# A recurrence with a mixture of experts on one core: the last two experts summed straight to 128 rows, the last weight loaded in two parts, the first output units in halves

## The chip, the cores and the metric

The kernel runs on one core of a Trainium2 chip. A core has five engines with instruction streams of their own: TensorE (PE, matmuls), VectorE (DVE), ScalarE (ACT), GpSimd (POOL) and SyncE (SP). They wait for one another by semaphores. Sixteen DMA engines move data between the memory outside (HBM) and the core's memory, of 128 partitions. Matmuls write to PSUM. The metric is the device time of one execution in microseconds (us), the median over several runs.

## The reference

Inputs are `x` and `f_logit` of shape (4, 5056, 256), a vector `lower_bound` of 256, `phi` (256 x 32), `w1` (8 x 256 x 1024) and `w2` (8 x 1024 x 256), all in fp32. The first part is a gated recurrence along the sequence, the second a soft mixture of 8 experts with 4 slots each:

```python
f = lower_bound + (1 - lower_bound) * sigmoid(f_logit)
for t in range(S):
    h = f[:, t] * h + (1 - f[:, t]) * x[:, t]
    y[:, t] = h
x = y.reshape(20224, 256)
logits = x @ phi                               # 20224 x 32
d = softmax(logits, axis=0)                    # over all tokens
slot_input = (d.T @ x).reshape(8, 4, 256)
slot_out[e] = relu(slot_input[e] @ w1[e]) @ w2[e]
c = softmax(logits, axis=1)                    # over the 32 slots
out = c @ slot_out                             # 20224 x 256
```

The slot inputs are sums over all tokens, so no output can be computed before the whole sequence has been read and all experts have run.

## The kernel before

The tokens are worked on in units: `n_grp` = 10 groups along the sequence, for each of `B` = 4 sequences, make 40 units of 512 tokens (448 in the units of the last group but one). In a unit a partition holds `R` = 4 neighbouring tokens, so one partition's piece of a unit in `out` is 4 KB in a row. The order of the instructions is written out by hand; each engine runs its own in that order.

**First stage** (the loop at L336). Units are loaded by SyncE, gated (ACT), multiplied (POOL), transposed (PE), scanned (DVE), transposed back and multiplied with `phi`. The exponentials of the logits stay on chip in `etall`, with one block of 32 partitions for each sequence b. Their weighted sum of tokens goes to `slot_ps`.

**Weights.** `load_w` (L104) issues the 16 weight loads on POOL, `w1` first and then `w2`, one expert each. POOL's DMAs read fp32 and write bf16: 1 MB read and 512 KB written for each load. `W_AT` (L111) says at which unit how many are issued; the last eight, all of `w2`, come at unit 36. In the built program a load waits for the landing of the load eight before it.

**Experts** (L411 to L489). `hid` (L416) holds the hidden activations, transposed, with 32 columns for each expert: the expert's own 4 slots are filled and the other 28 columns are zero. It is cleared by POOL (L417), after the loads in POOL's order, and filled from the transposes by ACT (L467, experts 0 to 3) and DVE (L469, experts 4 to 7). At L478 a loop over the experts and over the 8 chunks `fc` of 128 hidden values multiplies them with `w2`:

```python
nc.tensor.matmul(so4_ps[ds(fc % 4 * NS, NS), :], hid[:, fc, e], w2_sb[e][:, fc], ...)
```

The 32 rows of result go to one of four blocks of rows of `so4_ps`, by `fc % 4`. The four partial sums have then to be added, and the 32 rows repeated for the four sequences. That is what `rep` does: a matrix of 128 x 128 with a one wherever row and column agree modulo 32. DVE copies `so4_ps` to `so4` (L486), PE multiplies it with `rep` in fp32 (L488), and DVE divides by the softmax sums and writes `slot_out` in bf16 (L489): 128 rows, the 32 slots once for each sequence.

**Output** (L496 to L518). For each unit four matmuls (L502) take the 32 rows of its sequence and write four tokens for each partition to PSUM (`op`, four buffers). Then either DVE, in one instruction (L508), or ACT, in four (L514), multiplies with the reciprocal row sums `rrow` and writes `ob` (six buffers). Two counters, `load_dve` and `load_act`, say which of the engines takes a unit. SyncE issues one DMA of 512 KB for each unit (L516).

Of the kernel before, what the change touches and what calls it, by code (L numbers as in the profile page):

```python
# [10 lines left out]
BF16 = mybir.dt.bfloat16  # L11
AX = mybir.AxisListType
ALU = mybir.AluOpType
ACT = mybir.ActivationFunctionType
# [4 lines left out]
def kernel(  # L19
# [10 lines left out]
    nc = tc.nc  # L30
    B, S, D = x.shape
    E = moe_w1.shape[0]
    F = moe_w1.shape[2]
    NS = moe_phi.shape[1]
    SPE = NS // E
    P = 128
    DC = D // P
    FC = F // P
    R = 4
# [6 lines left out]
    def first(g):  # L46
        return g * G if g < n_grp - 1 else S - G
# [4 lines left out]
    def rows(g):  # L52
        return used(g) // R
# [41 lines left out]
    rrow = store.tile([P, n_grp, R, B], F32, name="rrow")  # L95
# [4 lines left out]
    w2_r = moe_w2.rearrange("e (p fc) d -> e p fc d", p=P)  # L100
    w1_sb = [store.tile([P, DC, F], BF16, name=f"w1_sb{e}") for e in range(E)]
    w2_sb = [store.tile([P, FC, D], BF16, name=f"w2_sb{e}") for e in range(E)]

    def load_w(i):  # L104
        if i < E:
            nc.gpsimd.dma_start(out=w1_sb[i], in_=w1_r[i])
        else:
            nc.gpsimd.dma_start(out=w2_sb[i - E], in_=w2_r[i - E])  # L108


    W_AT = {12: 1, 18: 1, 24: 1, 30: 1, 34: 3, 35: 1, 36: 8}  # L111
# [6 lines left out]
    with tc.tile_pool(name="ld", bufs=3) as ld, \  # L118
# [217 lines left out]
        for n in range(n_unit):  # L336
# [13 lines left out]
            else:  # L350
# [11 lines left out]
                for _ in range(W_AT.get(n, 0)):  # L362
                    load_w(w_next[0])
                    w_next[0] += 1
# [47 lines left out]
    with tc.tile_pool(name="ew", bufs=1) as ew, \  # L412
         tc.tile_pool(name="pm", bufs=2, space=PSUM) as pm, \
         tc.tile_pool(name="pbig", bufs=1, space=PSUM) as pbig:

        hid = ew.tile([P, FC, E, NS], BF16, name="hid")  # L416
        nc.gpsimd.memset(hid.rearrange("p f e s -> p (f e s)"), 0.0)  # L417
        rep2 = rep.rearrange("p b s -> p (b s)")

        sin_ps = pm.tile([P, DC, NS], F32, name="sin_ps", tag="pm")  # L420
        slot_v = slot_sb.rearrange("p (c o) -> p o c", o=DC)
        for o in range(DC):
            nc.tensor.matmul(sin_ps[:, o], slot_v[:, o], rep2[:, :NS],
                             start=True, stop=True, skip_group_check=True)
        sin = ew.tile([P, DC, NS], BF16, name="sin")
        for o in range(DC):
            nc.vector.tensor_scalar_mul(sin[:, o], sin_ps[:, o], omlb[:, ds(o, 1)])

        cs1 = ew.tile([P, 1], F32, name="cs1")
        nc.vector.tensor_reduce(cs1, csum, AX.X, ALU.add)  # L430


        Q = 4
        H = F // 2
        his = []
        for q in range(E // Q):
            hi = ew.tile([P, F], BF16, name=f"hi{q}")
            for k in range(2):
                hi_ps = (psu.tile([P, H], F32, name="hi_ps", tag="up") if q == 0 else
                         pbig.tile([P, H], F32, name="hi_ps", tag=f"hi_ps{k}"))  # L440
                for o in range(DC):
                    for j in range(Q):
                        nc.tensor.matmul(hi_ps[ds(j * NS, NS)], sin[:, o],
                                         w1_sb[q * Q + j][:, o, ds(k * H, H)],
                                         start=(o == 0), stop=(o == DC - 1),
                                         skip_group_check=True)
                if k == 0:
                    nc.scalar.activation(hi[:, ds(k * H, H)], hi_ps, ACT.Relu)
                else:
                    nc.vector.tensor_scalar_max(hi[:, ds(k * H, H)], hi_ps, 0.0)  # L450
            his.append(hi)
        cs_ps = pm.tile([P, 1], F32, name="cs_ps", tag="pm")
        nc.tensor.matmul(cs_ps, rep2, cs1, start=True, stop=True)
        for q in range(E // Q):
            ht_ps = psu.tile([P, FC, P], BF16, name="ht_ps", tag="up")
            hi_v = his[q].rearrange("p (c f) -> p f c", f=FC)
            for fc in range(FC):
                nc.tensor.transpose(ht_ps[:, fc], hi_v[:, fc], ident)

            src = ht_ps.rearrange("p f (j s) -> p f j s", s=NS)[:, :, :, ds(0, SPE)]  # L460
            src = bass.AP(tensor=src.tensor, offset=src.offset + q * Q * SPE,
                          ap=[list(src.ap[0]), [P, FC], [NS + SPE, Q], [1, SPE]])
            dst = hid[:, :, ds(q * Q, Q), ds(0, SPE)]
            dst = bass.AP(tensor=dst.tensor, offset=dst.offset + q * Q * SPE,
                          ap=[list(dst.ap[0]), [E * NS, FC], [NS + SPE, Q], [1, SPE]])
            if q == 0:
                nc.scalar.copy(dst, src)  # L467
            else:
                nc.vector.tensor_copy(dst, src)  # L469
        for g0, k in ((0, n_grp - 2), (n_grp - 2, 1), (n_grp - 1, 1)):  # L470
            n_p = rows(g0)
            nc.vector.reciprocal(rrow[:n_p, ds(g0, k)], rs_ps[:n_p, ds(g0, k)])
        rcs = ew.tile([P, 1], F32, name="rcs")
        nc.vector.reciprocal(rcs, cs_ps)


        so4_ps = pm.tile([P, D], F32, name="so4_ps", tag="pm")
        for e in range(E):  # L478
            for fc in range(FC):
                nc.tensor.matmul(so4_ps[ds(fc % 4 * NS, NS), :], hid[:, fc, e],  # L480
                                 w2_sb[e][:, fc],
                                 start=(e == 0 and fc < 4),
                                 stop=(e == E - 1 and fc >= FC - 4),
                                 skip_group_check=True)
        so4 = ew.tile([P, D], F32, name="so4")
        nc.vector.tensor_copy(so4, so4_ps)  # L486
        so_ps = pm.tile([P, D], F32, name="so_ps", tag="pm")
        nc.tensor.matmul(so_ps, rep2, so4, start=True, stop=True)  # L488
        nc.vector.tensor_scalar_mul(slot_out, so_ps, rcs)  # L489


# [1 line left out]
    with tc.tile_pool(name="pout", bufs=4, space=PSUM) as pout, \  # L493
         tc.tile_pool(name="osb", bufs=6) as osb:
        load_act = load_dve = 0.0
        for n in range(n_unit):  # L496
            g, b = divmod(n, B)
            n_p = rows(g)
            op = pout.tile([P, R, D], F32, name="op", tag="op")
            ew = etall[:, ds(g * G, n_p * R)].rearrange("s (p r) -> s p r", r=R)  # L500
            for r in range(R):
                nc.tensor.matmul(op[:n_p, r], ew[ds(b * NS, NS), :, r],  # L502
                                 slot_out[ds(b * NS, NS), :],
                                 start=True, stop=True, skip_group_check=True)
            ob = osb.tile([P, R, D], F32, name="ob", tag="ob")
            if load_dve + 1.2 <= load_act + 1.8:
                load_dve += 1.2
                nc.vector.tensor_tensor(  # L508
                    ob[:n_p], op[:n_p],
                    rrow[:n_p, g, :, ds(b, 1)].broadcast_to([n_p, R, D]), ALU.mult)  # L510
            else:
                load_act += 1.8
                for r in range(R):
                    nc.scalar.activation(ob[:n_p, r], op[:n_p, r], ACT.Copy,  # L514
                                         scale=rrow[:n_p, g, r, ds(b, 1)])
            nc.sync.dma_start(  # L516
                out=out[ds(b * S + first(g), n_p * R)].rearrange("(p r) d -> p r d", r=R),
                in_=ob[:n_p])  # L518


# [28 lines left out]
```

## Time and profile before

| | |
|---|---|
| time, median of 4 runs | 209.7 us (208.87 to 210.78) |
| the profiled execution | 210.78 us, with a span of 209.0 us |
| busy in that span | PE 134.9, DVE 146.5, ACT 133.3, POOL 95.8 us |
| moved by DMA | 71.26 MB; HBM read 58.75 MB, written 20.71 MB |
| last weight issued, landed | 127.84, 147.69 us |
| first output DMA issued | 153.03 us |
| last output landed | 207.69 us |

The span runs from the first to the last instruction; times inside it count from its start. The page gives the busy time of each engine, then the span in 40 equal slices (each digit a share in tenths), DMA queues, the chain of work that ended last, and the costliest groups. A line such as "L488" is that of the kernel before. In the timeline a row is start, length, engine, line, operation, what it writes and reads, shapes, how many, and in brackets the idle time before it with what ended it. A row of several instructions spans them all.

### The profile page before, as it was taken

How to read it: one execution, taken by the hardware profiler on the slowest of the kernel's cores; microseconds unless marked ns; L12 is line 12 of the kernel's file. 1: busy time of each engine (PE TensorE's matmuls, PEld its weight loads, DVE VectorE, ACT ScalarE, POOL GpSimd, SP SyncE). 2: the span in 40 equal slices, each digit the busy share in tenths (PEclk: the TensorE clock that was granted, in tenths of full speed). 3: DMA queues.
4: the chain of work that ended last, by engine and by line, in shares of the span. 5: the costliest groups of instructions: out<-in, count | busy, mean ns of one | idle time of the engine just before them, and what ended most of it. 6: DMA issues, size and time to landing. Idle time of an engine off the chain costs nothing.

```text
span 209.0 us, 3047 instructions
## 1 busy us (share of the span) xinstructions
PE 134.9 (65%) x1084; PEld 94.4 (45%) x1084; DVE 146.5 (70%) x159; ACT 133.3 (64%) x178; POOL 95.8 (46%) x64
## 2 busy tenths in 40 slices
PE   0658558665867497675868596983577578778400
PEld 0337437554755486554656474662233233334100
DVE  1677549999799979999997899632185555756420
ACT  3575599799888988899985981320074365454430
POOL 1555749976998198855998985000000000000000
PEclk9999787998899969999987999999555555555555
DMA  6999999999999999999999999999059999999995
GB/s 195 413 412 408 410 409 407 409 411 409 398 323 419 376 350 415 409 314 418 411 387 326 169 213 214 213 213 207 6 224 401 404 405 408 407 405 408 325 370 213
DMA packets 19550, 71.26 MB, mean 341 GB/s; under 512 B 2192, under 2 KB 2192, under 8 KB 19536
## 3 DMA queue, kind: packets, MB, share of 16 engines
q1 hardware_dynamic: 16944, 62.66, 75.9%
q0 software_dynamic: 2304, 8.39, 20.3%
q8 instruction: 8, 0.13, 0.2%
q10 hardware_dynamic: 288, 0.03, 0.1%
q14 instruction: 6, 0.05, 0.1%
HBM read 58.75 MB, written 20.71 MB: 380 GB/s over the span
## 4 chain that ended last, share of the span: by engine, by line
DMA 30%; PE 23%; DVE 21%; issue 9%; ACT 8%; POOL 3%; SPq 2%; DVEq 0%; ACTq 0%; POOLq 0%
DMA w_sb<-in_moe_w_dram 14%; DMA out_dram<-ob 13%; DVE h L196 11%; PE hp L207 8%; PE sp L164 6%; DVE ob L508 5%; PE up L164 4%; ACT s_t L148 4%; DVE ht L216 3%; DMA f_t<-in_f_logit_dram 3%; POOL u_t L159 2%; PE op L502 2%; ACT a L186 2%; ACT ob L514 2%; SPq L516 1%
## 5 line engine op out<-in xcount | busy, mean ns | idle before, releaser
L159 POOL TENSOR_TENSOR u_t<-s_t,x_t 128x1024 bf16<-128x1024 bf16 x39 | 83.1, 2156 | 26.1 <-ACT s_t L148 21.7
L196 DVE TENSOR_TENSOR_SCAN h<-a,h,up 128x512 bf16<-128x512 f32 (+1 forms) x72 | 86.1, 1249 | 7.0 <-PE up L164 4.4
L207 PE MATMUL hp<-ident_f,h 128*128 128x128 f32 (+1 forms) x160 | 32.2, 330 | 29.8 <-DVE ht L216 17.0
L186 ACT ACTIVATE a<-sp,nomlb 128x1024 f32<-128x1024 bf16 (+2 forms) x46 | 43.4, 995 | 12.4 <-PE sp L164 11.1
L514 ACT ACTIVATE ob<-op,rrow 128x256 f32<-128x256 f32 (+1 forms) x64 | 25.1, 475 | 36.0 <-DVE ob L508 19.2
L508 DVE TENSOR_TENSOR ob<-op,rrow 128x1024 f32<-128x1024 f32 (+1 forms) x24 | 29.0, 1223 | 20.4 <-DMA out_dram<-ob 14.7
L502 PE MATMUL op<-slot_out,etall 32*128 32x256 bf16 (+1 forms) x160 | 34.5, 402 | 11.7 <-ACT ob L514 8.1
L207 PEld LDWEIGHTS hp<-ident_f,h 128*128 128x128 f32 (+1 forms) x160 | 23.8, 210 | 40.3 <-DVE ht L216 21.7
L148 ACT ACTIVATE s_t<-f_t 128x2048 bf16<-128x2048 f32 (+1 forms) x23 | 38.8, 1690 | 4.3 <-DMA f_t<-in_f_logit_dram 3.2
L164 PE MATMUL sp<-ident_f,s_t 128*128 128x128 f32 x160 | 26.4, 314 | 9.8 <-ACT s_t L148 8.4
L164 PE MATMUL up<-ident_f,u_t 128*128 128x128 f32 x160 | 27.3, 297 | 4.0 <-POOL u_t L159 4.0
L502 PEld LDWEIGHTS <-etall 32*128 32x128 bf16 (+1 forms) x160 | 16.0, 133 | 30.5 <-issue 26.7
L164 PEld LDWEIGHTS sp<-ident_f,s_t 128*128 128x128 f32 x160 | 22.2, 165 | 11.1 <-issue 5.9
L164 PEld LDWEIGHTS up<-ident_f,u_t 128*128 128x128 f32 x160 | 20.8, 155 | 6.1 <-POOL u_t L159 5.4
L216 DVE COPY ht<-hp 128x512 f32<-128x512 f32 (+1 forms) x20 | 13.5, 673 | 6.0 <-PE hp L207 6.0
L216 ACT COPY ht<-hp 128x512 f32<-128x512 f32 (+1 forms) x19 | 11.1, 586 | 5.3 <-PE hp L207 5.3
L196 DVE TENSOR_TENSOR_SCAN h<-a,up 128x512 bf16<-128x512 f32 x8 | 9.3, 1208 | 1.2 <-PE up L164 1.2
L231 PE MATMUL lg<-h,phi 128*32 128x512 bf16 (+1 forms) x80 | 7.3, 413 | 0.0
L148 ACT ACT_TABLE_LOAD x4 | 5.1, 1283 | 1.7 <-PEq L533 1.7
L272 PE MATMUL slot_ps<-ht,et 128*32 128x256 bf16 (+1 forms) x144 | 6.1, 295 | 0.0
L480 PE MATMUL so_ps<-w_sb,hid 128*32 128x256 bf16 x64 | 2.7, 291 | 4.7 <-DMA w_sb<-in_moe_w_dram 4.7
L108 POOL DMA_DIRECT2D w_sb<-in_moe_w_dram x8 | 4.3, 555 | 2.5 <-DMA w_sb<-in_moe_w_dram 2.5
(58 smaller groups left out, 63.4 us busy)
## 6 DMA issues: line engine op xcount, KB each, us to landing
x_t<-in_x_dram SPq DMA_DIRECT2D x40, 512.0 KB, 9.8
out_dram<-ob SPq DMA_DIRECT2D x36, 512.0 KB, 6.0
f_t<-in_f_logit_dram SPq DMA_DIRECT2D x17, 1024.0 KB, 11.5
w_sb<-in_moe_w_dram POOLq DMA_DIRECT2D x16, 512.0 KB, 9.3
f_t<-in_f_logit_dram SPq DMA_DIRECT2D x6, 512.0 KB, 7.9
out_dram<-ob SPq DMA_DIRECT2D x4, 448.0 KB, 7.0
phi_f<-in_moe_phi_dram ACTq DMA_DIRECT2D x1, 32.0 KB, 5.1
lb<-in_lower_bound_dram ACTq DMA_DIRECT2D x1, 1.0 KB, 4.1
```

The lines of the kernel that those rows point to most:

```text
L148: nc.scalar.activation(sts[n // 2][:, ds(n % 2, k)], fs[n // 2][:, ds(n % 2, k)], ACT.Sigmoid, scale=-1.0)
L159: nc.gpsimd.tensor_tensor(uts[n], s_t, x_t, ALU.mult)
L164: nc.tensor.transpose(ps[:, :, r], t[:, r], ident_f)
L186: nc.scalar.activation(decays[n // 2, o][:, ds(n % 2, k), :T], sp[:, ds(n % 2, k), :T, o], ACT.Identity, scale=nomlb[:, ds(o, 1)], bias=1.0)
L196: nc.vector.tensor_tensor_scan(h[:, :T, o], decays[n // 2, o][:, n % 2, :T], up[:, :T, o], hs[n - B][:, ds(used(n // B - 1) - 1, 1), o] if ...
L207: nc.tensor.transpose(hp[:n_p, r], hw[:, :n_p, r], ident_f)
L216: copy(hts[g][:n_p, b].rearrange("p r d -> p (r d)").bitcast(F32), hps.pop(n)[:n_p].rearrange("p r c -> p (r c)"))
L231: nc.tensor.matmul(lg[ds(b * NS, NS), :], phi[:, o], hs[g * B + b][:, :T, o], start=o == 0, stop=o == DC - 1, skip_group_check=True)
L272: nc.tensor.matmul(slot_ps[ds(b * NS, NS), :], et[:n_p, r, b], ht[:n_p, b, r], start=(g == 0 and r == 0), stop=(g == n_grp - 1 and r == R ...
L502: nc.tensor.matmul(op[:n_p, r], ew[ds(b * NS, NS), :, r], slot_out[ds(b * NS, NS), :], start=True, stop=True, skip_group_check=True)
L508: nc.vector.tensor_tensor(ob[:n_p], op[:n_p], rrow[:n_p, g, :, ds(b, 1)].broadcast_to([n_p, R, D]), ALU.mult)
L514: nc.scalar.activation(ob[:n_p, r], op[:n_p, r], ACT.Copy, scale=rrow[:n_p, g, r, ds(b, 1)])
```

## The change

Four things are different.

1. **The last two experts (W = 2)** no longer go through `so4_ps`. A new tile `wide` holds their hidden activations with 128 columns instead of 32, the expert's 4 slots at the same place in each of the four blocks. It is cleared by POOL behind `hid`, and filled by two more copies on ACT. The matmuls of these two experts write all 128 rows of `so_ps` directly, 8 chunks each, accumulating on top of the product of `rep` and `so4`, which now covers experts 0 to 5 and comes ahead of them in PE's order. The copies of experts 6 and 7 to `hid` are still made; nothing reads them.
2. **The last weight** is loaded by two DMAs, of four chunks each.
3. **The first two output units** are each made in two halves of two tokens for each partition: the first by DVE, the second by ACT, each with a DMA of its own of 256 KB.
4. The counters that divide the units between DVE and ACT begin at the third unit.

```diff
-            nc.gpsimd.dma_start(out=w2_sb[i - E], in_=w2_r[i - E])
+            k = FC // 2 if i == 2 * E - 1 else FC
+            for c in range(0, FC, k):
+                nc.gpsimd.dma_start(out=w2_sb[i - E][:, ds(c, k)],
+                                    in_=w2_r[i - E][:, ds(c, k)])
...
+        W = 2
+        wide = ew.tile([P, FC, W, B, NS], BF16, name="wide")
+        nc.gpsimd.memset(wide.rearrange("p f w b s -> p (f w b s)"), 0.0)
...
+            for w in range(W):
+                e = E - W + w
+                if e // Q == q:
+                    src = ht_ps[:, :, ds((e % Q) * NS + e * SPE, SPE)]
+                    nc.scalar.copy(wide[:, :, w, :, ds(e * SPE, SPE)],
+                                   src.unsqueeze(2).broadcast_to([P, FC, B, SPE]))
...
-        for e in range(E):
+        for e in range(E - W):
...
-        nc.tensor.matmul(so_ps, rep2, so4, start=True, stop=True)
+        nc.tensor.matmul(so_ps, rep2, so4, start=True, stop=False, skip_group_check=True)
+        for w in range(W):
+            for fc in range(FC):
+                nc.tensor.matmul(so_ps, wide[:, fc, w].rearrange("p b s -> p (b s)"),
+                                 w2_sb[E - W + w][:, fc],
+                                 start=False, stop=w == W - 1 and fc == FC - 1,
+                                 skip_group_check=True)
         nc.vector.tensor_scalar_mul(slot_out, so_ps, rcs)
...
+            if n < 2:
+                by_vector(0, R // 2)
+                nc.sync.dma_start(out=dst[:, ds(0, R // 2)], in_=ob[:n_p, ds(0, R // 2)])
+                by_scalar(R // 2, R // 2)
+                nc.sync.dma_start(out=dst[:, ds(R // 2, R // 2)],
+                                  in_=ob[:n_p, ds(R // 2, R // 2)])
+                continue
```

`by_vector(r, k)` is the DVE instruction of L508 on `k` of the four tokens from `r` on, and `by_scalar(r0, k)` the ACT instructions of L514 on `k` of them.

More of the change, by code (lines that the diff above doesn't have):

```diff
@@ L482 @@
                                  start=(e == 0 and fc < 4),
-                                 stop=(e == E - 1 and fc >= FC - 4),
+                                 stop=(e == E - W - 1 and fc >= FC - 4),
                                  skip_group_check=True)
@@ L505, with by_vector, by_scalar @@
             ob = osb.tile([P, R, D], F32, name="ob", tag="ob")
+            dst = out[ds(b * S + first(g), n_p * R)].rearrange("(p r) d -> p r d", r=R)
+            def by_vector(r, k):
+                nc.vector.tensor_tensor(
+                    ob[:n_p, ds(r, k)], op[:n_p, ds(r, k)],
+                    rrow[:n_p, g, ds(r, k), ds(b, 1)].broadcast_to([n_p, k, D]), ALU.mult)
+            def by_scalar(r0, k):
+                for r in range(r0, r0 + k):
+                    nc.scalar.activation(ob[:n_p, r], op[:n_p, r], ACT.Copy,
+                                         scale=rrow[:n_p, g, r, ds(b, 1)])
+            if n < 2:
[5 more added lines that the diff above has]
+                continue
             if load_dve + 1.2 <= load_act + 1.8:
                 load_dve += 1.2
-                nc.vector.tensor_tensor(
-                    ob[:n_p], op[:n_p],
-                    rrow[:n_p, g, :, ds(b, 1)].broadcast_to([n_p, R, D]), ALU.mult)
+                by_vector(0, R)
             else:
                 load_act += 1.8
[L513 to L518, printed above, removed]
+                by_scalar(0, R)
+            nc.sync.dma_start(out=dst, in_=ob[:n_p])
 _INS = ['x', 'f_logit', 'lower_bound', 'moe_phi', 'moe_w1', 'moe_w2']
```

## The prediction

> **What bounds the kernel now.** I read the clock and DMA rows of the 40 slices first, then the chain of work that ended last, then the timeline and one-microsecond windows of the stretch that the diff touches.
>
> ```profile
> PEclk9999787998899969999987999999555555555555
> DMA  6999999999999999999999999999059999999995
> GB/s 195 413 412 408 410 409 407 409 411 409 398 323 419 376 350 415 409 314 418 411 387 326 169 213 214 213 213 207 6 224 401 404 405 408 407 405 408 325 370 213
> ```
>
> A slice is 209.0 / 40 = 5.2 us. The transfer engines are full from start to end, except for one hole: slice 29 (146.3 to 151.5 us) is at 0, slice 30 at 5. Before the hole only weights move (213 GB/s written, as they are read in fp32 and land in bf16); after it only the output (405 GB/s). The hole is what the change can shorten. At its edge the TensorE clock falls to half.
>
> ```profile
> 127.84 19.85 DMA w_sb<-in_moe_w_dram
> 147.69 0.04 issue
> 147.73 0.64 PE so_ps L480 x8
> 148.38 0.02 issue
> 148.40 0.43 DVE so L486
> 148.83 0.04 issue
> 148.88 1.24 PE so_ps L488 x2
> 150.11 0.02 issue
> 150.14 0.50 DVE slot_out L489
> 150.63 0.04 issue
> 150.68 1.08 PE op L502 x16
> 151.75 0.02 issue
> 151.78 3.50 DVE ob L508 x3
> ```
>
> This is the chain (start, length, what). The last weight lands at 147.69, and `slot_out` needs 2.95 us more. The output's first DMA is issued at 153.03 (timeline, L516). From there the chain is output transfers: the second bound.
>
> ```profile
> 145.00:146.00 1.00, 0.08 (x4) 0.08 (x7) 0.00 (x0) 0.00 (x0) 0.00 (x0) 1.00 1.06 213
> 146.00:147.00 1.00, 0.32 (x8) 0.12 (x8) 0.00 (x0) 0.00 (x0) 0.00 (x0) 0.60 0.30 57
> 147.00:148.00 1.00, 0.27 (x8) 0.14 (x7) 0.00 (x0) 0.00 (x0) 0.00 (x0) 0.50 0.04 8
> ```
>
> The last three columns are clock, DMA share and GB/s. Most of the 16 DMA engines finish by about 146.3; a few laggards hold the landing until 147.69.
>
> ```profile
> 145.92 0.40 PE L480 MATMUL so_ps<-w_sb,hid 128*32 128x256 bf16 x8 [2.68 <-DMA w_sb<-in_moe_w_dram]
> 147.73 0.62 PE L480 MATMUL so_ps<-w_sb,hid 128*32 128x256 bf16 x8 [1.41 <-DMA w_sb<-in_moe_w_dram]
> 159.76 1.01 PE L502 MATMUL op<-slot_out,etall 32*128 32x256 bf16 x4 [0.33 <-DVE ob L508]
> ```
>
> Eight 32-column matmuls take 0.40 us at full clock and 0.62 at half, because four run side by side. Four matmuls on the same array rows (third line) take 1.01 at half clock: a pitch of (1.01 - 0.40) / 3 = 0.20.
>
> **What the Trainium skill says.** "TensorE: Matmul & The Clock Gate", section "What's actually happening": the clock is full or half by recent activity, in free-running windows of 3.41 us. The trace agrees: full until 146.19, half to the end; the window before that is 20% busy (0.40 of e5's matmuls and 0.27 of e6's, over 3.41). Same page, "The mechanism": small matmuls on different array tiles overlap. The trace agrees: 40 at L480 take 1.28 us. So 128-column ones, which fill the array, must go one by one. "DMA: Bandwidth & Descriptors", "Latency and other measured facts": two of the 16 engines are usually slower under GpSimd-issued loads. The windows above agree. Same page, "Why small descriptors are slow (HBM only)": about 3 cycles are fixed per packet. No run here shows 2 KB packets.
>
> **The change part by part.**
>
> *The sum of the last experts.* Removed from behind the last weight: the copy (0.43), the fp32 matmul (1.24), and e7's own packed matmuls (0.64), with gaps 2.41 us from 147.73 to 150.14. The copy and the fp32 matmul now follow e5, which lands at 142.8; its matmuls are done by 143.24 (timeline, L480), the copy by 143.7, the fp32 matmul by 145.0 even at half clock. That is ahead of e6's 145.92; if it were late, e6 would be pushed by the excess. Added: 16 full-array matmuls of 256 columns; four of them have to follow the last landing.
> At half clock these four take 1.01 (the L502 row). So the end comes at 147.73 + 1.01 = 148.74 instead of 150.11: gain 1.37.
> At full clock the pitch is (1.28 - 0.28) / 9 = 0.11 from the ten rounds of four at L480, so four take 0.33 + 0.28 = 0.61: end 148.34, gain 1.77.
> The pitch holds only if the PE has finished the 12 earlier ones by 147.73. If e6 is seen at 145.92, as here, and the clock halves at 146.19, three start at 0.11 and 13 at 0.20: the end is near 149.2, gain 0.9. But e6's landing was late in this trace: landings are 2.4 to 2.5 us apart (140.30, 142.80), then 3.08, then 1.82; at the usual distance it is 145.25, and its eight (0.77 + 0.28 = 1.05) end at 146.35 at full clock. I take 1.37.
>
> *Last weight in two loads.* Bytes are equal. Each of the laggards has eight half-size packets less for the first half, half of a load's 2.46 us, so it lands about 1.2 us earlier, at 146.5; its four matmuls (1.01) are done by 147.5, just in time. GpSimd issues 17 loads instead of 16. By the built program each waits for the load eight before it; so the seventeenth waits for the ninth, which lands at 130.0. Queued behind it on GpSimd are the memset of `hid` (1.82 us, from 128.36) and the new one of `wide`, the same size. They now end near 130.6 + 2 x 1.82 = 134.2; the first user, the `hid` copy, comes at 140.42. Cost nothing, 6 us of cover; beyond it they would delay the expert sum.
>
> *Copies into `wide`.* Two more on ACT of 128 values each, 0.27 by the L467 row. They wait for the DVE's `hid` copy (until 141.39) and end near 142. ACT has nothing else until 151.8, and only e6's matmuls wait for them. Nothing.
>
> *Halves of the first two units.* A DVE half is 512 values: 0.69 (the 128x512 PSUM row L450) against 1.22. The built program raises the PE semaphore only at a unit's fourth matmul, so the half waits as long as before (1.1 us from 150.68 to 151.78). First issue: 0.53 earlier. But ACT's half waits for the DVE's half of the same tile, then takes 0.36 + 0.47 = 0.83 (two of L514), so the second DMA is issued 0.90 after the first. Bytes follow an issue by 0.84 (153.03 to 153.87 in the trace); half a unit keeps the queue busy 0.64 (512 KB / 405 GB/s / 2). Hole: 0.90 - 0.64 = 0.26. Afterwards: second unit's halves at +1.3 and +1.7, unit 2 at +2.1, all earlier than the queue needs them. Net gain 0.53 - 0.26 = 0.27; bounds 0 and 0.53. Two more output issues on SyncE (0.35 each) lie inside the queue's backlog.
>
> *Smaller packets.* A half has 128 packets of 2 KB instead of 4. With an excess x over half a 4 KB packet (159 ns here, in the trace's packet records), each DMA engine pays 16 x for the weight and 32 x for four output halves: 48 x. The skill's 3 cycles against 2048 / 32 = 64 beats give an estimate of 78 x 3 / 64 = 4 ns, so 0.2 us; lower end 0, as equal bytes can't go faster than full engines. The 256-byte packets of `phi` take 18 ns here, so x above 18 ns would be surprising: upper end 0.9 us. I take 0.
>
> Sum at half clock: 1.37 + 0.27 = 1.64. After the first byte the output is transfer-bound (windows at share 1.0 from 154 to 206), so the whole gain reaches the end. The profiled execution took 210.78 for a span of 209.0: it becomes 207.4 in span, 209.1 in all. The median shown is 209.7, the profiled run being the slowest of four; from the median, 209.7 - 1.6 = 208.1.
>
> **The rivals.**
> *Full clock kept.* With e5, the fp32 matmul and e6's eight full-array ones in it, the window that decides is over 50% busy instead of 20%; adding up the timeline's matmuls in the trace's other windows, those of 0.50 and less were mostly followed by half clock, of 0.51 and more by full. Against: the phase is free, and e7 still waits. Gain 1.77 + 0.27 + about 0.45 for `op` (0.61 instead of 1.08) = 2.5: 207.2.
> *The serial matmuls become the bound.* Half clock early and e6 late: gain 0.9 + 0.0 to 0.27, 208.7. For it: this very trace has both.
> *Slower: fixed cost of a packet.* If a 2 KB packet costs nearly what a 4 KB one does, 48 x eats the gain from x = 1.64 / 48 = 34 ns. At x = 80 ns the cost is 3.8 us: net 2.2 slower, 211.9. Against: weight packets with twice the HBM bytes take twice as long, so cost goes by bytes.
> *It doesn't do what it says.* The output halves wait for whole units (above), so that part is nearly void already: it stays in my sum at 0.27.
>
> **How the numbers follow.** Half clock, forecast 0.46; full clock 0.28; PE-bound 0.21; packets 0.05. Range: from the full-clock case less 0.4 for a spread of the runs that is itself 1.9 us wide, 206.8, to the PE-bound case with the packet estimate and the same spread, 209.4. About 1% (2.1 us) is what a measurement of this kernel can tell from no change: faster by more needs 207.6 or less, nearly all of the full-clock case and a tail of the forecast, 0.31. Slower by more is the packet case, 0.04. The rest is 0.65.
>
> **What would show it.** Chain after: last weight landing at about 147.7, then four matmuls, `slot_out` and `op`, no L498 or L500. First output issue near 151.1. A short dip of the DMA share within a microsecond of the first bytes. Wrong if the second half lands later than 148, if PE runs without a stop from e6 to e7, if the clock differs at 146 to 150, or if output GB/s falls in the first slices.

## The result, and the profile after

The changed kernel takes 209.81 us (median of 35 runs, 207.9 to 211.72); the kernel before, over 56 runs, 210.62 us (208.16 to 213.07). The ratio is 0.9975, with a 95% interval of 0.9953 to 0.9998: 0.5 us faster, by 0.04 to 1.0. A ratio, here and below, is that of the means of the fast runs, those within 1.5% of the fastest of the same kernel, so it is not the quotient of the two medians. The forecast was 1.6 us faster. The larger sample of the kernel before lies 0.9 us above the median that the prediction started from; the ratio applied to that median gives 209.2, but the measured 209.81 is outside the stated range.

The profiled execution took 209.54 us with a span of 207.8. The slices of its page:

```profile
PEclk9999999999999969999997999999855555555555
DMA  5999999999999999999999999999179999999993
GB/s 192 416 409 412 409 412 406 409 409 412 404 304 420 379 346 416 407 315 421 409 391 338 209 214 213 214 215 194 34 289 396 409 406 409 405 405 405 335 379 154
```

The hole is narrower, but one slice ahead of it has changed too: slice 28 moved 194 GB/s, where its predecessors moved 209 to 215 and the same slice before 207. The chain of work that ended last, from the last weight on:

```profile
129.36 18.52 DMA w_sb<-in_moe_w_dram
147.88 0.04 issue
147.92 0.61 PE so_ps L503 x4
148.53 0.03 issue
148.56 0.49 DVE slot_out L507
149.05 0.04 issue
149.09 1.08 PE op L520 x16
150.17 0.04 issue
150.21 2.42 DVE ob L527 x3
```

As drawn up in the prediction, four matmuls stand between the last landing and `slot_out`, and the copy and the fp32 matmul are gone from the chain. They take 0.61, the full-clock figure. The first output DMA is issued at 150.92 instead of 153.03. Where a part of this went is seen one step earlier, in the windows of one microsecond (last columns: clock, DMA share, GB/s) and in PE's rows of the timeline. The first window is the kernel before, the next three the changed one:

```profile
144.00:145.00 1.00, 0.00 (x0) 0.00 (x0) 0.00 (x0) 0.00 (x0) 0.00 (x0) 1.00 1.07 213
```

```profile
143.00:144.00 1.00, 0.70 (x2) 0.40 (x3) 0.04 (x1) 0.00 (x0) 0.00 (x0) 1.00 1.06 199
144.00:145.00 1.00, 0.40 (x4) 0.36 (x4) 0.00 (x0) 0.00 (x0) 0.00 (x0) 1.00 1.04 139
145.00:146.00 1.00, 0.63 (x6) 0.42 (x5) 0.00 (x0) 0.00 (x0) 0.00 (x0) 1.00 1.08 195
```

```profile
144.60 1.03 PE L503 MATMUL so_ps<-w_sb,wide 128*128 128x256 bf16 x8 [0.81 <-DMA w_sb<-in_moe_w_dram]
146.67 0.60 PE L503 MATMUL so_ps<-w_sb,wide 128*128 128x256 bf16 x4 [1.03 <-DMA w_sb<-in_moe_w_dram]
147.92 0.60 PE L503 MATMUL so_ps<-w_sb,wide 128*128 128x256 bf16 x4 [0.66 <-DMA w_sb<-in_moe_w_dram]
```

The DMA engines are busy all the time (the packets of one engine overlap by some 20 ns in the records, so a full share can read above 1.0), yet for a microsecond they move 139 GB/s instead of 213. Expert 6 is seen at 144.60, expert 7's second half at 147.92: 3.3 us for the last load, where the one before it took 2.44. In this execution the earlier stages were 0.7 us ahead (expert 5 landed at 142.12 instead of 142.79), and the last weight still landed 0.2 us later than before.

### The profile page after: what moved, and what is told of

Same layout as the page of the kernel before. It is cut to its first block, busy times and chain, and to the rows that moved or that the text cites. A ratio compares the mean times of both kernels' runs of the same rounds, so it can differ in the third digit from the quotient of the medians.

```text
span 207.8 us, 3060 instructions
## 1 busy us (share of the span) xinstructions
PE 134.8 (65%) x1084; PEld 95.1 (46%) x1084; DVE 145.9 (70%) x160; ACT 133.5 (64%) x180; POOL 98.0 (47%) x66
## 4 chain that ended last, share of the span: by engine, by line
DMA 32%; DVE 18%; PE 13%; ACT 9%; issue 7%; SPq 3%; POOL 1%; DVEq 0%; ACTq 0%; POOLq 0%
DMA out_dram<-ob 13%; DMA w_sb<-in_moe_w_dram 13%; DVE h L199 10%; DMA f_t<-in_f_logit_dram 6%; DVE ob L527 5%; PE hp L210 5%; ACT s_t L151 5%; PE sp L167 3%; DVE ht L219 3%; PE up L167 3%; SPq L549 3%; ACT ob L533 2%; PE lg L234 1%; ACT a L189 1%; ACT ht L219 1%
## 5 line engine op out<-in xcount | busy, mean ns | idle before, releaser
L527 DVE TENSOR_TENSOR ob<-op,rrow 128x1024 f32<-128x1024 f32 (+2 forms) x25 | 29.0, 1180 | 21.3 <-DMA out_dram<-ob 17.2
L520 PE MATMUL op<-slot_out,etall 32*128 32x256 bf16 (+1 forms) x160 | 33.9, 401 | 12.1 <-ACT ob L533 9.8
L167 PE MATMUL sp<-ident_f,s_t 128*128 128x128 f32 x160 | 26.9, 318 | 9.8 <-ACT s_t L151 8.7
L110 POOL DMA_DIRECT2D w_sb<-in_moe_w_dram x9 | 4.8, 557 | 3.7 <-DMA w_sb<-in_moe_w_dram 3.7
```

Of the source, the lines that this page charges most:

```text
L167: nc.tensor.transpose(ps[:, :, r], t[:, r], ident_f)
L520: nc.tensor.matmul(op[:n_p, r], ew[ds(b * NS, NS), :, r], slot_out[ds(b * NS, NS), :], start=True, stop=True, skip_group_check=True)
L527: nc.vector.tensor_tensor(ob[:n_p, ds(r, k)], op[:n_p, ds(r, k)], rrow[:n_p, g, ds(r, k), ds(b, 1)].broadcast_to([n_p, k, D]), ALU.mult)
```

## Experiments

Changes in us are the ratio's distance from 1 times 210.6. The interval from expert 5's landing to the last landing is read from the landing records of the trace, since expert 5's load ends ahead of nearly all that is changed here; a load has sixteen such records, one for each DMA engine, and has landed with the last of them. In the kernel before the interval is 4.90, in the changed kernel 5.76.

**The three parts one by one.** First, the kernel before with only the split load:

```diff
-            nc.gpsimd.dma_start(out=w2_sb[i - E], in_=w2_r[i - E])
+            k = FC // 2 if i == 2 * E - 1 else FC
+            for c in range(0, FC, k):
+                nc.gpsimd.dma_start(out=w2_sb[i - E][:, ds(c, k)],
+                                    in_=w2_r[i - E][:, ds(c, k)])
```

> The kernel before with only the last weight in two loads. Theory S: 5.8 us instead of 4.9 from expert 5's first matmul to the first that needs the second half; ratio 1.003 to 1.004. Rival C, and the prediction's step (packets cost by bytes): 4.9, ratio 1.000.

Ratio 1.0040 (1.0013 to 1.0067): 0.85 us slower. PE's rows of its timeline:

```profile
142.44 0.40 PE L483 MATMUL so_ps<-w_sb,hid 128*32 128x256 bf16 x8 [0.43 <-DMA w_sb<-in_moe_w_dram]
144.87 0.40 PE L483 MATMUL so_ps<-w_sb,hid 128*32 128x256 bf16 x8 [2.03 <-DMA w_sb<-in_moe_w_dram]
146.76 0.41 PE L483 MATMUL so_ps<-w_sb,hid 128*32 128x256 bf16 x4 [1.49 <-DMA w_sb<-in_moe_w_dram]
148.01 0.40 PE L483 MATMUL so_ps<-w_sb,hid 128*32 128x256 bf16 x4 [0.85 <-DMA w_sb<-in_moe_w_dram]
```

From expert 5 to expert 6 2.43, to the first half 1.89 more, to the second 1.25: 5.57 in all. Nothing else was changed here, so this is against rival C, scatter; the six profiles with this split, counted below, put it out.

Second, the kernel before with only the halves of the first two output units (the change's last part, as in its diff):

> The kernel before with only the first two output units in halves. The prediction's step: 0.27 faster, ratio 0.9987. By the profiles so far: first output DMA 2.4 us after slot_out instead of 2.9, 4 MB moved 11.8 us after it instead of 11.5: net 0.1 to 0.2, ratio 0.999 to 1.000.

Ratio 0.9969 (0.9944 to 0.9995): 0.65 us faster, 0.1 to 1.2. The forecast 0.27 is inside.

Third, the direct sum alone, twice. It is the changed kernel with these two lines:

```diff
-            k = FC // 2 if i == 2 * E - 1 else FC
+            k = FC
...
-            if n < 2:
+            if n < 0:
```

> The changed kernel with the last weight in one load and all output units whole: only the direct sum of experts 6 and 7 is left. Theory S (the split load lands later) and theory H (the halves lengthen the output) together: from expert 5's first matmul to expert 7's first 4.9 us, as before (5.8 in the changed kernel); eight matmuls behind the landing, 1.05 at full clock or 1.8 at half, against 2.38 before; from the first output DMA to the last landing 54.7, as before (55.6 changed). Gain over before 0.6 to 1.3 us, ratio 0.994 to 0.997, better than the changed kernel. Rival C (both intervals only scatter from run to run): the intervals don't go with the edits, and the ratio is above the changed kernel's 0.9975.

> The direct sum alone (one load, whole units), once more, beside the kernel that also has the halves. The profiles price the halves at 0.4 to 0.5 us gained up to the first output DMA and 0.3 lost in the queue: then it stands 0.1 to 0.2 us behind the one with halves, ratio 0.994 to 0.997. If the first readings (0.9986 against 0.9941) were right, it stands 0.9 behind.

Ratios 0.9986 (0.9956 to 1.0017) and 0.9942 (0.9915 to 0.9968): 0.3 and 1.2 us faster, 0.76 on the mean. From expert 5's to the last landing it took 4.87 and 5.23. The three parts add up, as far as intervals of half a microsecond either way can tell: 0.85 - 0.65 - 0.76 = -0.56, against -0.53 for the whole change.

**Taking one part away.** The changed kernel with `k = FC`, so with one load, twice:

> The changed kernel with the last weight in one load. Theory S: from expert 5's first matmul to expert 7's first 4.9 us instead of 5.8, then eight matmuls in 1.05 (full clock) instead of four in 0.6; a net gain of 0.4 over the changed kernel, ratio to before 0.996. The output, still in halves, takes 55.6 from the first DMA to the last landing. Rival C: the first interval stays at 5.8 or scatters, and the kernel is 0.4 slower than the changed one.

> The changed kernel with the last weight in one load, once more. If the split is what ate the gain, the ratio to before is 0.993 to 0.996 again, ahead of the changed kernel's 0.9975; from expert 5's landing to the last landing 4.9 us. If the first reading (0.9941) was scatter, 0.997 or more.

Ratios 0.9941 (0.9917 to 0.9965) and 0.9933 (0.9908 to 0.9957): 1.2 and 1.4 us faster than before, more than twice what the whole change gives. Both are what theory S, that the split load lands later, had forecast. The second one's profile:

```profile
145.07 1.03 PE L503 MATMUL so_ps<-w_sb,wide 128*128 128x256 bf16 x8 [0.17 <-DMA w_sb<-in_moe_w_dram]
147.57 1.03 PE L503 MATMUL so_ps<-w_sb,wide 128*128 128x256 bf16 x8 [1.47 <-DMA w_sb<-in_moe_w_dram]
```

Expert 7 comes 2.50 behind expert 6, and now eight matmuls follow the landing, 1.03 instead of 0.60. The split saves these 0.43 and costs 0.8 in landing (on the mean of the profiles, below).

The changed kernel with all output units whole (`if n < 0`):

> The changed kernel with all output units whole. Theory H: the first output DMA comes 0.5 us later than in the changed kernel after slot_out, but from there to the last landing it is 54.7 instead of 55.6 us, so the kernel is 0.4 faster than the changed one, ratio to before 0.996. The split load is kept: 5.8 us from expert 5's first matmul to the first behind the second half. Prediction's step (halves worth 0.27): 0.3 slower than the changed kernel, ratio 0.999.

Ratio 0.9968 (0.993 to 1.0005), no difference from the changed kernel that could be told. Its split weight again took long, 5.69 from expert 5's landing. By the parts it should be 0.1 slower than before (0.85 - 0.76); it measures 0.7 faster, from 1.5 faster to 0.1 slower. So the parts add up to about half a microsecond, and no better.

**Only one expert direct.** `W = 1` and one load:

```diff
-            k = FC // 2 if i == 2 * E - 1 else FC
+            k = FC
...
-        W = 2
+        W = 1
```

> The changed kernel with one load for the last weight and only expert 7 summed straight (W = 1), so that eight full-array matmuls follow the fp32 one instead of sixteen. Where the clock is full and the experts start in time it costs and gains nothing against W = 2: expert 6 lands 2.5 us ahead of expert 7, enough for the copy and the fp32 matmul. Theory L (where PE is late or its clock is half, the sixteen in a row are the bound, as in the run of the direct sum alone): 0.2 to 0.8 us ahead of W = 2, ratio 0.991 to 0.994. Rival: same as W = 2.

Ratio 0.9935 (0.9908 to 0.9961): the same as with W = 2 and one load. The rival holds; theory L isn't seen in the time, though the situation it speaks of occurs. In the profiled run of the direct sum alone, PE was late:

```profile
144.78 1.49 PE L492 MATMUL so_ps<-w_sb,hid 128*32 128x256 bf16 x48
146.81 0.70 PE L500 MATMUL so_ps<-so,rep 128*128 128x256 f32 x2 [0.53 <-DVE so L498]
147.34 1.91 PE L503 MATMUL so_ps<-w_sb,wide 128*128 128x256 bf16 x16
```

The sum begins 4 us later than in the kernel before (140.98), after three windows of half clock between 119 and 143 us (granted clock in the trace), and the sixteen matmuls run without a stop past the landing at 146.91: `slot_out` starts 2.38 behind it. With W = 1 the sum began as late, at 145.10, and `slot_out` started 1.81 behind the landing. So what theory L describes is there in the profiles, 0.6 us of it, and too rare or too small to show in the times; and the experts' stage has less cover than the profile of before showed.

**What makes the second half late.** First, is it the number of loads, or the small packets? The last weight in two loads of 64 partitions each:

```diff
-            k = FC // 2 if i == 2 * E - 1 else FC
-            for c in range(0, FC, k):
-                nc.gpsimd.dma_start(out=w2_sb[i - E][:, ds(c, k)],
-                                    in_=w2_r[i - E][:, ds(c, k)])
+            k = P // 2 if i == 2 * E - 1 else P
+            for c in range(0, P, k):
+                nc.gpsimd.dma_start(out=w2_sb[i - E][ds(c, k)],
+                                    in_=w2_r[i - E][ds(c, k)])
```

> The changed kernel, but the last weight's two loads take 64 partitions each with all eight chunks, so that packets keep 4 KB; all eight matmuls of expert 7 then need both. Theory P (the half-size packets are what delays the landing): from expert 5's landing to the last landing 4.9 us, as with one load. Rival N (a seventeenth load costs, whatever its packets): 5.7 us, as in the changed kernel.

4.91: no delay. Ratio 0.9952 (0.9924 to 0.9979). Its windows have no dip until the loads run out:

```profile
143.00:144.00 1.00, 1.00 (x41) 0.98 (x44) 0.86 (x2) 0.43 (x2) 0.00 (x0) 1.00 1.07 213
144.00:145.00 1.00, 0.47 (x21) 0.18 (x9) 0.90 (x5) 0.00 (x0) 0.00 (x0) 1.00 1.03 205
145.00:146.00 1.00, 1.00 (x7) 0.81 (x8) 0.00 (x0) 0.00 (x0) 0.00 (x0) 1.00 0.67 135
```

So it isn't the seventeenth load. All eight loads of `w2` in halves (`k = FC // 2`):

> The changed kernel with all eight loads of w2 in two halves, 24 loads in all. Theory P (a steady price of each small packet): eight times the 0.8 us of one split weight, so w2 takes 26 us instead of 19.7 from the last landing of w1 to its own last, and the kernel is 5 us slower than the changed one. Rival Q (a price paid once, where the packet size changes): w2 takes 20.5 us, and the kernel is within 0.5 us of the changed one.

From the last landing of `w1` to the last of `w2` 21.66 us, against 20.0 to 20.65 with whole loads (20.4 on the mean) and 20.7 to 21.6 where the last weight is split. Neither number was met: it is 1.2 us longer than with whole loads, where theory P has 6.3 and rival Q 0.8. Theory P falls. Most halves follow each other at 1.25 us, half of 2.46 and 0.02, which makes 0.3 us over sixteen halves; most of the rest is one burst of slow packets:

```profile
129.00:130.00 1.00, 0.24 (x2) 0.27 (x3) 1.00 (x3) 0.00 (x0) 0.28 (x1) 1.00 1.14 205
130.00:131.00 1.00, 1.00 (x11) 0.43 (x11) 1.00 (x1) 0.00 (x0) 0.24 (x1) 1.00 1.13 164
131.00:132.00 1.00, 1.00 (x35) 0.91 (x32) 1.00 (x2) 0.68 (x2) 0.53 (x1) 1.00 0.93 113
132.00:133.00 1.00, 1.00 (x15) 0.36 (x7) 0.87 (x2) 0.46 (x1) 0.00 (x0) 1.00 1.13 209
```

In the trace's packet records of the changed kernel, too, 42 of the 256 small weight packets are slow, nearly all of them between 144 and 145 us; the others take 173 ns, where a 4 KB one takes 324. The ratio of the kernel with all of `w2` in halves was 0.9991 (0.9954 to 1.0028).

I then took it that the burst comes once, where 2 KB packets begin. Two kernels put that beginning elsewhere: all sixteen weights in halves (`w1` too, by its two parts `o`), and the first weight of `w2` split in place of the last (`if i == E`).

> The changed kernel with all sixteen weight loads in two halves, 32 loads of 2 KB packets. Theory T (the price is paid once, about a microsecond after 2 KB packets begin among 4 KB ones): no such change is left near the end, so from expert 5's last landing to the last landing it is 4.9 us as with whole loads, and the four last matmuls still follow 0.6 behind: ratio to before 0.990 to 0.994. Rival U (small weight packets are slow now and then, wherever they are): 5.0 to 5.8 us, w2 takes 21.5 us or more, ratio 0.998 or more.

> The changed kernel with the first weight of w2 in two loads instead of the last. Theory T: the burst of slow packets comes a microsecond after the first 2 KB packets, near 129 us, and w2 as a whole takes 0.8 us longer than with whole loads (20.9 instead of 20.1 from the last landing of w1); 4.9 us from expert 5's landing to the last one. Theory V (it is the end of the queue, where no further load stands behind, that is slow): no burst, 20.1.

With all in halves it took 5.01 from expert 5's to the last landing, with no burst near the end; but bursts came between 116 and 125 us, `w1` landed at 128.73 (126.5 to 128.3 elsewhere), and the ratio was 0.9983 (0.9954 to 1.0013). With the first weight of `w2` split there was no burst at all, 4 slow packets, 20.54 us for `w2`. So theory T falls as well: the beginning of small packets alone isn't it. Theory V, the end of the queue, was left, and two kernels tested it: expert 6's weight split in place of expert 7's (`2 * E - 2`), and the changed kernel with a further load behind the last weight, which nothing reads (seven of eight chunks, as the on-chip memory has no room for all eight):

```diff
+    spare = store.tile([P, FC - 1, D], BF16, name="spare")
...
+            if i == 2 * E - 1:
+                nc.gpsimd.dma_start(out=spare, in_=w2_r[0][:, ds(0, FC - 1)])
```

> The changed kernel with expert 6's weight in two loads and expert 7's in one. Theory V: no burst, or a smaller one, since a whole load stands behind; 4.9 us from expert 5's landing to the last landing. Rival W': small packets late in the load are slow: 5.6 us.

> The changed kernel with one more load behind the last weight: seven of the eight chunks of the first weight of w2 once more, into a tile that nothing reads. It adds 2.2 us of transfer behind the weights that nothing waits for but the first outputs on the same engines. Theory V (the end of the load queue makes the small packets slow): no burst, 4.9 us from expert 5's landing to that of the second half of expert 7. Rival W (it is this weight, or the small packets, wherever the queue ends): burst and 5.6 to 5.8 us as in the changed kernel.

The further load changes nothing: 51 slow packets, and 5.49 us from expert 5's landing to that of the second half. Its window has the same dip as the changed kernel's:

```profile
143.00:144.00 1.00, 1.00 (x17) 0.65 (x10) 0.53 (x1) 0.58 (x1) 0.00 (x0) 1.00 1.04 197
144.00:145.00 1.00, 0.95 (x17) 0.78 (x19) 0.17 (x1) 0.27 (x1) 0.00 (x0) 1.00 1.09 137
145.00:146.00 1.00, 1.00 (x40) 0.97 (x44) 0.90 (x2) 0.43 (x2) 0.00 (x0) 1.00 1.07 188
```

Theory V falls too. Expert 6's weight in halves showed no slow packet, and its halves landed 2.49 after expert 5. The last landing nevertheless was 5.60 behind expert 5's: the packets of expert 7 ended at 147.02, and the landing was seen 0.90 later, which is another matter (see the end).

The size of the delay is settled, its cause is not. With the last weight split into chunks, and the other weights whole, the burst came in all six profiles and the last half landed 5.49 to 6.05 us behind expert 5, 5.69 on the mean. With that weight in one load, leaving out the run with expert 6 split, it was 4.85 to 5.23, 4.93 on the mean: 0.8 us. Half of it is common to all DMA engines: the middle one of the sixteen needs 5.13 to 5.43 us with the split (5.30 on the mean) and 4.88 to 4.95 without (4.91). That is about what the burst costs each engine, 0.2 to 0.4 us in the six profiles. The rest is that the last engine ends further behind the middle one, by 1.4 us instead of 1.1; why isn't known.

What starts the burst stays open: it isn't the number of loads, a steady price of 2 KB packets, their beginning, or the end of the queue alone. Nor is it the fetching of instructions. The trace has 16 KB packets of an instruction queue, 0.9 us each. In four of the six profiles one of them starts at 143.5 to 143.7, just ahead of the burst, but with the further load it came at 147.84 and with both halves by the DVE at 146.17, and the burst was at 143 to 145 as in the others.

**The halves of the output.** Both halves by the DVE:

```diff
-                by_scalar(R // 2, R // 2)
+                by_vector(R // 2, R // 2)
```

> The changed kernel with both halves of the first two units made by the DVE, so that no half waits for ACT behind the DVE. Theory H1 (the queue runs dry between the first two halves): 4 MB of output are moved 11.5 us after the first output DMA, as with whole units, instead of 11.8. Rival H2 (the small packets cost it): 11.8 stays.

The second half's DMA now follows the first by 0.59 us instead of 0.88, as the output DMA issues of the changed kernel and then of this one show:

```profile
150.92 0.35 SPq L538 DMA_DIRECT2D out_dram<-ob  x1
151.80 0.34 SPq L540 DMA_DIRECT2D out_dram<-ob  x1
```

```profile
150.91 0.35 SPq L538 DMA_DIRECT2D out_dram<-ob  x1
151.50 0.56 SPq L540 DMA_DIRECT2D out_dram<-ob  x1
```

By the packet records, 4 MB are out 11.8 us after the first issue, as in the changed kernel, and 11.5 with whole units. So H2 is met in its number. But the packet records show both causes. The DMA engines still stood idle between the first two halves, for 0.15 us on the mean of the sixteen, where it was 0.2 in the changed kernel and 0.02 with whole units: 0.59 is too long as well. And a 2 KB packet of the output took 86 ns on the mean, half a 4 KB one 82; for 32 of them that is 0.1 us. Ratio 0.9972 (0.9941 to 1.0003), as the changed kernel's.

The halves computed as in the changed kernel, but sent in one DMA for each unit, in place of the two DMAs:

```diff
+                by_scalar(R // 2, R // 2)
+                nc.sync.dma_start(out=dst, in_=ob[:n_p])
```

> The changed kernel with the first two units still computed in halves on DVE and ACT, but one DMA of 4 KB packets each. The first DMA comes 0.9 us later than in the changed kernel, when ACT is done; 4 MB take 11.5 us from it. Ratio to before 0.999 to 1.000: behind both the changed kernel and the one with whole units.

First issue 3.34 us after `slot_out` starts, against 2.37; 4 MB in 11.5. Ratio 1.0004 (0.9967 to 1.0041), as expected.

**The end of the output.** In the changed kernel's profile the output took 55.64 us from the first issue to the last landing, before 54.66. The windows at the end, of before and then of after:

```profile
206.00:207.00 1.00, 0.00 (x0) 0.00 (x0) 0.00 (x0) 0.00 (x0) 0.00 (x0) 0.50 0.46 184
207.00:208.00 1.00, 0.00 (x0) 0.00 (x0) 0.00 (x0) 0.00 (x0) 0.00 (x0) 0.50 0.04 16
```

```profile
204.00:205.00 1.00, 0.00 (x0) 0.00 (x0) 0.00 (x0) 0.00 (x0) 0.00 (x0) 0.50 0.48 193
205.00:206.00 1.00, 0.00 (x0) 0.00 (x0) 0.00 (x0) 0.00 (x0) 0.00 (x0) 0.50 0.06 25
206.00:207.00 1.00, 0.00 (x0) 0.00 (x0) 0.00 (x0) 0.00 (x0) 0.00 (x0) 0.50 0.01 4
```

A share of 0.06 is one of sixteen engines. Here one engine landed 1.3 us after the other fifteen (206.56 and 205.28), and 0.7 us of this execution's gain went to it. Does that belong to the change? The kernel before, unchanged, twice:

> The kernel before, profiled once more. From the first output DMA to the last landing it took 54.7 us in its first profile, and 55.6 in the changed kernel's, of which 0.3 is in the first 4 MB. Theory Y (the rest is scatter of the last packets of one DMA engine): anything from 54.0 to 55.7. Theory Z (the changed kernel's output tail is longer): 54.0 to 54.8 again.

> The kernel before, a third profile, for the same question. Theory Y: anything from 54.0 to 55.7. Theory Z: 54.0 to 54.8 again.

54.68 and 55.33: scatter of the kernel before reaches nearly as far (the profiles of all the experiments lie between 53.99 and 55.68), so a single 55.64 says nothing. By the packet records 99% of the bytes were out 52.7 to 53.1 us after the first issue where units left whole, and 53.1 to 53.4 where the first two left in halves. What scatters is the last 1%, from 0.9 to 2.1 us. So theory Z isn't borne out, though a difference of a few tenths in that last 1% isn't excluded.

## Why the prediction was wrong

*The last weight in two loads: "Cost nothing".* This step failed. The prediction reasoned that equal bytes take equal time, gave GpSimd's part 6 us of cover, and asked when the first half would land, at 146.5 (it was 146.62). It took for granted that the second would land where the whole weight had. It landed 0.8 us later on the mean of six profiles, and alone the split costs 0.85 us (0.3 to 1.4), half of the forecast gain. The prediction's own sign, a second half later than 148, did not show it: this execution was 0.7 us ahead, so that the landing came at 147.88.

The packet term was the right place to look: 16 x for the weight, x being what a 2 KB packet takes over half a 4 KB one, with an upper end of 18 ns for x. The six thousand ns by which 42 packets of the changed kernel were slow, spread over 256, are 23 ns each on the mean, beyond that end; 16 of them make 0.4 us, which is the half of the delay that all engines share. But a fixed cost for each packet was the wrong model for it. Such a cost there is, and it is no larger than the 4 ns that the prediction estimated from the Trainium skill ("DMA: Bandwidth & Descriptors", "Why small descriptors are slow (HBM only)"): outside the bursts, halves of eight packets for each engine ended 1.253 us apart by the packet records, where whole loads took 2.458, so (1.253 - 1.229) / 8 = 3 ns, and a part of this is the closing packet of 22 ns that each half has to itself. The delay comes with the burst, of which that section says nothing.

*The laggards.* The prediction read from the windows that a few engines finish late, and put it to engines that are usually slower under loads from GpSimd. The packet records of before show something else. Up to 134 us the last engine of each load landed within 0.7 us of the middle one. At 134.28 and at 143.83 two 16 KB packets of an instruction queue start, 0.94 us each, and at just these two times one engine each stops moving weights, for 0.93 and 0.92 us. Two engines then land the last weight at 147.66 and 147.69, 1.0 behind the middle one. Such a packet came between 133.0 and 135.3 in all 20 profiles, and at expert 5's landing the last engine was 0.8 to 1.3 us behind the middle one in all of them. So in the kernel before, the landing that bounds this stage is that of engines which have fetched instructions on the way.

*The direct sum: 1.37.* The mechanism was right: four matmuls in 0.61, nothing of L498 and L500 in the chain. From the last landing to `slot_out` it takes 0.68 instead of 2.45, 1.77 less, as in the full-clock case. But neither figure holds for every execution. In five profiles with the old sum it is 2.45, 2.31, 2.20, 2.23 and 1.71. The fp32 matmul ran at half clock in the first four, as in the first row below (the kernel before with the split), and at full clock in the fifth (the kernel before with the halves):

```profile
148.94 1.22 PE L491 MATMUL so_ps<-so,rep 128*128 128x256 f32 x2 [0.53 <-DVE so L489]
```

```profile
145.48 2.02 PE L480 MATMUL so_ps<-w_sb,hid 128*32 128x256 bf16 x64
148.03 0.70 PE L488 MATMUL so_ps<-so,rep 128*128 128x256 f32 x2 [0.53 <-DVE so L486]
```

In the seven profiles with the direct sum of two experts and the last weight split it is 0.68 five times, 0.91 and 1.54: 2.18 on the mean against 0.84, or 1.34 less. So the size of this term was right as well, by these few profiles. With four matmuls more behind the landing it is 1.11 or 1.12 in five profiles, 1.94 at half clock (the row below, from the first profile of the changed kernel with one load) and 2.38 where PE was late: 1.41 on the mean, 0.77 less than 2.18. The 0.76 measured for the direct sum alone (0.3 and 1.2) fits that.

```profile
148.93 1.86 PE L503 MATMUL so_ps<-w_sb,wide 128*128 128x256 bf16 x8 [0.34 <-DMA w_sb<-in_moe_w_dram]
```

So the shortfall is in the main the split: 1.34 for the tail and 0.2 for the halves, less 0.8 at the landing, leave about 0.8, an estimate from few profiles, inside the measured 0.04 to 1.0.

*The rivals.* The clock did stay full until 149.2, as the second case of the prediction had it, and its 1.77 for the tail came; its 0.45 for `op` did not, as the clock fell when `op` began (1.06), and the split took 0.8 back. The PE-bound case is seen in four of the fifteen profiles with the direct sum (tails of 0.91, 1.54, 1.81 and 2.38). The slower rival named the right resource, small packets, and the wrong size and form; it needed 34 ns on every half packet, and the output's halves paid 4. The prediction's rule for the clock, that windows from 0.51 on are mostly followed by full clock, holds in the trace of before up to the output; in the output stage, by the same count, twelve windows of 0.55 to 0.95 were followed by half clock.

*The halves: 0.27.* Confirmed within what can be measured: 0.52 earlier from `slot_out` to the first issue (2.89 to 2.37), 0.3 lost in the first 4 MB, 0.1 to 1.2 faster in the timed runs. That the 0.3 agrees with the prediction's 0.26 is in part luck: the hole that it named is 0.2, and the packets, which it took at nothing, are 0.1.

*Memsets, copies into `wide`, the DVE's order.* As forecast: `hid` was ready by 131.7 and `wide` by 133.4, the first copy came at 140.19, the new ones took 0.43 from 141.27.

*The end.* The claim that "the whole gain reaches the end" can't be read from one profile, and the times are too wide to prove it for the mean. A single profile can lose 0.7 us to the last engine, and gain 0.7 in the first stage; the difference of the two spans, 1.2 us, is no measure of the change.

## What to carry to other kernels

When a wait on a transfer bounds the stage, price an edit of that transfer by measuring its last landing alone, before anything is built on it: cutting the last load for an earlier start made its own end later, and keeping it whole gave 1.2 to 1.4 us instead of 0.5. When a removed tail is priced from one profile, ask in which states it is met: here the old tail took 1.71 to 2.45 us and the new one 0.68 to 1.54, by the clock and by how early PE came. When a wait ends with the last of sixteen engines, look at what held that one up. Where parts of a change can each be built alone, build them: here the signs of the parts differed, and their sum matched the whole.

## What was not expected of the hardware

- A 512 KB load in two halves of 2 KB packets (4 KB read, 2 KB written) moved 137 to 166 GB/s for a microsecond (144 to 145 us) instead of 213, and its end came 0.6 to 1.1 us late, in all six profiles with the last weight so split; in halves by partition, with 4 KB packets, it did not.
- A landing can be seen late: with expert 6 split, the last weight's packets ended at 147.02 and the landing was at 147.92, 0.90 us later, against 0.3 to 0.6 us in the other profiles.
- A 16 KB packet of instructions stops the weight packets of one DMA engine for 0.9 us (0.93 and 0.92 in the kernel before), and the last landing waits for that engine.
- The sum of the experts started at 140.6 to 141.5 us in the six profiles without a window of half clock from 112 us to there (all of `w2` in halves aside, where GpSimd clears `hid` later), and at 144.8 to 145.5 in the four with three or more. Where weights landed later that cost nothing; in three profiles with the direct sum `slot_out` came 0.7 to 1.3 us later behind the last landing (1.54 for 0.68, 1.81 and 2.38 for 1.11).
